# A GEGLU layer in seven block products: thirteen column pairs in place of twelve, four pairs' first products made ahead, some weight sums on GpSimd

## The chip, the cores and the metric

The kernel runs on one core of one Trainium2 chip. The metric is the time of one execution in microseconds (us); lower is better. Beside it stands the *span* of the profile, from the first to the last instruction that the trace shows. Three engines matter: TensorE (PE; its weight loads are PEld), VectorE (DVE) and ScalarE (ACT). GpSimd (POOL) is idle in the kernel before, but for 0.7 us at the start.

## The reference, cut to what matters

```python
B, S, D, F = 32, 32, 1024, 3584          # 1024 tokens in all, bf16
def reference(x, w_gate, w_up, w_down):
    return (gelu_tanh(x @ w_gate) * (x @ w_up)) @ w_down
```

## The kernel before

A product of 2 x 2 blocks is usually eight block products. The Winograd form needs seven, and some sums of blocks. The kernel uses it in the first layer (tokens in two halves of 512, D in two halves, two column tiles of 128 as a *pair*) and in the second.

- Products 1 and 2 use unsummed blocks in bf16. Products 3 to 7 use sums, kept as fp32r, a four-byte float type. Every matmul is 128x128 by 512 columns. A *slot* is one product, four matmuls. Matmuls write to PSUM, a memory of eight *banks*, of 512 columns each here; the other tiles lie in SBUF.
- A pair (gate and up) takes 14 products, 56 matmuls: 16 in bf16, 40 in fp32r. Without sums it would take 64.
- Four of 28 column tiles are computed directly, in two passes of 64 matmuls, one per half of the tokens. The second pass is *cover*: VectorE makes the sums of x meanwhile.
- `at=` is no time on the chip. It only sorts each engine's queue. TensorE's queue stands in program order. Waits on semaphores follow from reads and writes of the tiles.

```python
        KO = 2
        for h in range(2):                       # the direct tiles: one pass per half
            ...                                  # 64 matmuls each, then GELU and product
        # sums of x: DVE; the unsummed block S4 is converted by ACT
        sums_x(0, 21)
        sums_x(1, 23.5)
        sums_x(2, 26)
        sums_x(3, 28)
        sums_x(4, 32)
        ...                                      # the five weight blocks of pair 0
        for p in range(NP):                      # NP = 12
            ...
            product(1, 0, A[0], True)            # product n, gate (0) or up (1), PSUM bank
            act(bank(B[0]), bank(A[0]), COPY, at(1))
            product(1, 1, A[1], True)
            act(bank(B[1]), bank(A[1]), COPY, at(2))
            product(5, 0, E[0], True)
            act(p5[0], bank(E[0]), COPY, at(3))
            product(2, 0, A[0], False)
            act(g11, bank(A[0]), GELU, at(4))
            product(2, 1, A[1], False)
            glu(ml, 0, g11, bank(A[1]), at(5.2))
            product(6, 0, B[0], False)
            act(bank(C[0]), bank(B[0]), COPY, at(6))
            product(6, 1, B[1], False)
            act(bank(C[1]), bank(B[1]), COPY, at(7))
            product(5, 1, E[1], True)
            ...                                  # products 7, 3, 7, 3, 4, 4; adds, GELUs, products
            if p + 1 < NP:                       # weight sums of the next pair, all but one on DVE
                for u in range(3):
                    sums_w(p + 1, u, at(0.5 + 1.5 * u + (5.5 if p == 0 else 0)))
                sums_w(p + 1, 3, at(8.5))
                sums_w(p + 1, 4, at(7 if p else 9.05))
        ...                                      # second layer: seven sweeps of 56 matmuls
```

## Time and profile before

| | before |
|---|---|
| time, median (range of 4 runs) | 277.11 us (276.85 to 277.46) |
| span of the profiled run | 275.9 us |
| matmuls with the weights (bf16 + fp32r) | 432 + 760 |

First, the page's busy table (share of the span, number of instructions) and its chain of work that ended last.

```profile
## 1 busy us (share of the span) xinstructions
PE 270.6 (98%) x1191; PEld 184.4 (67%) x1208; DVE 208.2 (75%) x234; ACT 118.1 (43%) x180; POOL 0.7 (0%) x6
...
## 4 chain that ended last, share of the span: by engine, by line
PE 95%; DMA 2%; issue 1%; SPq 0%; DVE 0%
```

TensorE binds. The matmul records are long (0.38 to 0.40 us) and overlap, so their sum is no cost. Weight loads are the better ruler. There is one for each matmul, none is missing (1208), and the order of the program says which one belongs to which product. Counted so, an undisturbed bf16 matmul takes 0.2158 us (the second pass: 64 in 13.81 us), and an fp32r one 0.2267 us (a sweep of the second layer: 56 in 12.69 us). This is the ruler for all stage times. After a wait the first loads run a little ahead of their matmuls, so a stage border is good to about 0.2 us. Where fp32r products give way to bf16 ones the shift is regular: in a later pair the loads of the first product take 0.66 us, not 0.86, and those of the last product of the pair in front 1.13, not 0.91.

Next, the weight loads in order of time: start, length, and in brackets the idle time before with what ended it. Of the tiles, `arena` holds x and unsummed weights, `S` the sums of x, `T` those of the weights, `tmp` intermediates, `hT` the hidden layer; `ps` is PSUM. The four lines at the top are the first pass (the fourth runs on into what follows), the next four the first pair, the last is product 5 of the second pair.

```profile
4.58 1.44 PEld L117 LDWEIGHTS ps<-arena 128*128 128x128 bf16 x8 [0.28 <-issue]
6.69 1.41 PEld L117 LDWEIGHTS ps<-arena 128*128 128x128 bf16 x8 [0.67 <-DMA arena<-in_w_gate_dram]
8.75 1.42 PEld L117 LDWEIGHTS ps<-arena 128*128 128x128 bf16 x8 [0.64 <-issue]
10.75 23.87 PEld L117 LDWEIGHTS ps<-arena 128*128 128x128 bf16 x112 [0.58 <-issue]
...
34.73 0.86 PEld L117 LDWEIGHTS ps<-S,T 128*128 128x128 f32 x4
36.02 1.41 PEld L117 LDWEIGHTS ps<-arena 128*128 128x128 bf16 x8 [0.42 <-ACT ps L117]
...
44.23 0.76 PEld L117 LDWEIGHTS ps<-S,T 128*128 128x128 f32 x4 [0.35 <-DVE tmp L117]
45.43 0.77 PEld L117 LDWEIGHTS ps<-S,T 128*128 128x128 f32 x4 [0.44 <-DVE tmp L117]
...
47.99 0.87 PEld L117 LDWEIGHTS ps<-S,T 128*128 128x128 f32 x4
```

The groups of eight in the first pass start 2.0 to 2.1 us apart where eight matmuls need 1.73: TensorE waits for first data. In pair 0 it waits once for a ScalarE copy and twice for VectorE. At the start VectorE has the sums of two pairs to make. Product 5 of pair 0 starts at 34.73 us and that of pair 1 at 47.99: 13.26 us, where later pairs repeat every 12.61. So the first pair loses 0.65 us. Its 13.46 us in the ledger below hold 0.2 more, because it follows bf16 matmuls and lacks the head start of a later pair.

Then the busy time by window: length, then busy us of each engine with its instructions, clock, DMA share and GB/s. The windows are pair 0, pair 1 and pair 2.

```profile
core 0: us, PE busy (x) PEld busy (x) DVE busy (x) ACT busy (x) POOL busy (x), PEclk, DMA share, GB/s
...
33.00:46.46 13.46, 13.40 (x57) 8.85 (x56) 13.32 (x16) 10.05 (x15) 0.00 (x0) 1.00 0.29 78
46.46:59.08 12.62, 12.55 (x56) 8.92 (x57) 10.61 (x14) 6.93 (x11) 0.00 (x0) 1.00 0.67 177
59.08:71.68 12.60, 12.53 (x56) 8.92 (x56) 10.06 (x13) 6.93 (x11) 0.00 (x0) 1.00 0.43 137
```

In pair 0 VectorE is busy 13.32 of 13.46 us. In a later pair TensorE has the time to itself: 12.61 us, where 56 matmuls at cadence are 12.52.

Last, two groups of instructions: out<-in, shapes, count, busy us, mean ns.

```profile
L117 PE MATMUL ps<-S,T 128*128 128x512 f32 x480 | 118.4, 400 | 0.0
...
L117 DVE TENSOR_TENSOR T<-arena,T 128x1024 fp32r<-128x1024 bf16 x38 | 46.2, 1222 | 11.5 <-PE ps L117 11.1
```

One weight sum on VectorE is 1.22 us. The Trainium skill (VectorE: DVE Perf Modes, "The TRN2 errata") gives (N+151)/0.96 ns for an fp32 add of two tensors, checked there at N = 512 and 2048. My estimate from it for N = 1024 is 1224 ns. The trace agrees (1222), for a difference of bf16 blocks written as fp32r.

### The profile page before, as it was taken

What the parts mean: (1) busy time and instruction counts of PE and PEld (TensorE: products, weight loads), DVE (VectorE), ACT (ScalarE), POOL (GpSimd) and SP (SyncE); (2) the same over time, 40 slices, a digit from 0 to 9 for tenths busy, and PEclk for the clock granted to TensorE, in tenths of its full rate; (3) what the DMA queues carried; (4) which work ended last, traced back from release to release, by engine and by line L of the source; (5) the groups of instructions that cost most, each with busy time, mean ns of one, the idle gap of its engine ahead of it and who ended that gap; (6) DMA issues with size and microseconds to landing.
All of it is one profiled execution on the core that took longest, in us unless ns stands there. A gap on an engine that the chain in (4) does not pass through costs nothing.

```text
span 275.9 us, 3173 instructions
## 1 busy us (share of the span) xinstructions
PE 270.6 (98%) x1191; PEld 184.4 (67%) x1208; DVE 208.2 (75%) x234; ACT 118.1 (43%) x180; POOL 0.7 (0%) x6
## 2 busy tenths in 40 slices
PE   8999999999999999999999999999999999999995
PEld 3344466767686867677676868674447888888884
DVE  1049799896969678887969696269971999999942
ACT  2030484646454645556464546431121122245551
POOL 1000000000000000000000000000000000000000
PEclk9999999999999999999999999999999999999999
DMA  7999550593082029006700700194011000001112
GB/s 160 253 222 295 147 142 2 155 318 99 0 238 69 0 58 249 0 0 163 183 0 0 229 2 0 50 333 151 0 38 38 0 2 0 1 0 61 38 57 76
DMA packets 44815, 26.42 MB, mean 96 GB/s; under 512 B 8448, under 2 KB 44800, under 8 KB 44800
## 3 DMA queue, kind: packets, MB, share of 16 engines
q1 hardware_dynamic: 42576, 24.25, 32.2%
q10 hardware_dynamic: 2224, 1.97, 2.9%
q8 instruction: 9, 0.15, 0.2%
q14 instruction: 6, 0.05, 0.1%
HBM read 22.28 MB, written 2.10 MB: 88 GB/s over the span
## 4 chain that ended last, share of the span: by engine, by line
PE 95%; DMA 2%; issue 1%; SPq 0%; DVE 0%
PE ps L117 95%; DMA arena<-in_x_dram 2%; SPq L117 0%; DVE arena L117 0%
## 5 line engine op out<-in xcount | busy, mean ns | idle before, releaser
L117 PE MATMUL ps<-S,T 128*128 128x512 f32 x480 | 118.4, 400 | 0.0
L117 PEld LDWEIGHTS ps<-S,T 128*128 128x128 f32 x480 | 90.0, 188 | 21.5 <-DVE tmp L117 0.8
L117 PE MATMUL ps<-arena 128*128 128x512 bf16 x306 | 71.1, 379 | 1.4 <-DMA arena<-in_w_gate_dram 0.2
L117 ACT ACTIVATE tmp<-ps 128x512 f32<-128x512 f32 x64 | 38.3, 598 | 69.7 <-PE ps L117 69.5
L117 PEld LDWEIGHTS ps<-arena 128*128 128x128 bf16 x320 | 29.2, 98 | 39.9 <-issue 4.4
L117 ACT ACTIVATE ps<-ps 128x512 f32<-128x512 f32 x56 | 32.4, 581 | 52.6 <-PE ps L117 50.2
L117 DVE TENSOR_TENSOR T<-arena,T 128x1024 fp32r<-128x1024 bf16 x38 | 46.2, 1222 | 11.5 <-PE ps L117 11.1
L117 DVE TENSOR_TENSOR T<-arena 128x1024 fp32r<-128x1024 bf16 x38 | 45.8, 1217 | 7.4 <-PE ps L117 7.4
L117 PE MATMUL ps<-T,S 128*128 128x512 f32 x224 | 51.3, 390 | 0.0
L117 PEld LDWEIGHTS ps<-T,S 128*128 128x128 f32 x224 | 42.0, 188 | 8.8
L117 DVE TENSOR_TENSOR tmp<-ps,tmp 128x512 f32<-128x512 f32 x48 | 32.9, 689 | 12.9 <-PE ps L117 12.9
L117 DVE TENSOR_TENSOR hT<-tmp,ps 128x512 bf16<-128x512 f32 x32 | 21.8, 684 | 19.8 <-PE ps L117 19.8
L117 PE MATMUL ps<-arena,hT 128*128 128x512 bf16 x109 | 24.0, 379 | 0.2
L117 PEld LDWEIGHTS ps<-arena,hT 128*128 128x128 bf16 x112 | 10.9, 98 | 13.2 <-issue 0.3
L117 DVE TENSOR_TENSOR hT<-tmp 128x512 bf16<-128x512 f32 x24 | 16.6, 692 | 2.5
L117 ACT ACTIVATE tmp<-tmp 128x512 f32<-128x512 f32 x24 | 15.1, 632 | 6.9 <-DVE tmp L117 6.0
L117 DVE TENSOR_TENSOR S<-hT 128x1024 fp32r<-128x1024 bf16 x14 | 16.5, 1217 | 0.0
L117 PE MATMUL ps<-S 128*128 128x512 f32 x56 | 12.9, 389 | 0.0
L117 ACT ACTIVATE T<-arena 128x1024 fp32r<-128x1024 bf16 x12 | 12.6, 1053 | 0.0
L117 PEld LDWEIGHTS ps<-S 128*128 128x128 f32 x56 | 10.5, 188 | 2.2
L117 ACT ACTIVATE S<-arena 128x1024 fp32r<-128x1024 bf16 x9 | 9.3, 1055 | 3.2 <-PE ps L117 3.0
L117 ACT ACTIVATE S<-hT 128x1024 fp32r<-128x1024 bf16 x7 | 7.2, 1056 | 5.5 <-PE ps L117 5.5
(23 smaller groups left out, 48.3 us busy)
## 6 DMA issues: line engine op xcount, KB each, us to landing
arena<-in_w_gate_dram SPq DMA_DIRECT2D x12, 512.0 KB, 5.3
arena<-in_w_up_dram SPq DMA_DIRECT2D x12, 512.0 KB, 7.1
arena<-in_w_down_dram SPq DMA_DIRECT2D x4, 1536.0 KB, 8.3
out_dram<-arena SPq DMA_DIRECT2D x12, 128.0 KB, 1.7
arena<-in_w_down_dram SPq DMA_DIRECT2D x4, 256.0 KB, 6.6
arena<-in_w_up_dram ACTq DMA_DIRECT2D x4, 128.0 KB, 5.4
arena<-in_w_gate_dram ACTq DMA_DIRECT2D x2, 256.0 KB, 5.7
arena<-in_w_up_dram ACTq DMA_DIRECT2D x2, 256.0 KB, 6.2
```

Source lines behind the costliest of these rows:

```text
L117: ins = name(eng, *args, **kw) if callable(name) else getattr(eng, name)(*args, **kw)
```

## The change

Two direct tiles become a thirteenth pair. That would leave half the cover for the sums of x, so products 1 and 2 of four pairs run ahead of the pairs: those of pairs 0 and 1 inside the first pass, those of pairs 2 and 3 as 32 matmuls after a shorter second pass. Product 1 alone is needed later, so ScalarE saves its PSUM bank to SBUF (`kept`, in tiles of the hidden layer not written yet) before product 2 is added, and restores it when the pair comes. These four *early* pairs then have 10 slots, the nine *late* ones 14. GpSimd makes the first weight sum of each next pair, and in late pairs the third too. Two intermediates move from SBUF to PSUM. The matmuls with the weights go from 1192 to 1184.

```diff
-        BASE, PAIR = 32.0, 12.6
-        NP = 12
+        LEFT = [11, 12] + list(range(11))
+        NP, EARLY = len(LEFT), 4
+        kept = [hT[:, m:m + 2, :].rearrange("p t n -> p (t n)").bitcast(FP32).rearrange("p (j n) -> p j n", j=2)
+                for m in (7, 9, 22, 24)]
...
+            if k == 3 and m < 2:
+                act(kept[m][:, j, :], bank(2 * m + j), COPY, 10.5)
...
+        for p in (2, 3):
+            at = 25.8 + (p - 2) * 3.46
+            g, u = 2 * p, 2 * p + 1
+            for b, j, k0 in ((g, 0, 0), (u, 1, 0), (g, 0, 4), (u, 1, 4)):
+                for k in range(k0, k0 + 4):
+                    mm(b, stat(p, j, k), x0[:, k, :], k == 0, k in (3, 7), add=k > 3)
+                if k0 == 0:
+                    act(kept[p][:, j, :], bank(b), COPY, at + 0.9 * (j + 1))
+            act(tmp[:, p, :], bank(g), GELU, at + 2.7)
+            tt(hT[:, left(p), 0:512], tmp[:, p, :], bank(u), MUL, at + 3.6)
...
-        sums_x(4, 32)
+        sums_x(4, 22)
...
+            if p < EARLY:
+                o = -4
+                for j in range(2):
+                    act(bank(B[j]), kept[p][:, j, :], COPY, at(0.1 + j * 0.1))
+                product(5, 0, E[0], True)
+                act(p5[0], bank(E[0]), COPY, at(1))
+                product(5, 1, E[1], True)
+                product(6, 0, B[0], False)
+                act(bank(C[0]), bank(B[0]), COPY, at(3))
+                act(p5[1], bank(E[1]), COPY, at(3.1))
+                product(6, 1, B[1], False)
+                act(bank(C[1]), bank(B[1]), COPY, at(4))
...
+            u22 = bank(A[1] if p < EARLY - 1 else E[1])
...
-                for u in range(3):
-                    sums_w(p + 1, u, at(0.5 + 1.5 * u + (5.5 if p == 0 else 0)))
-                sums_w(p + 1, 3, at(8.5))
-                sums_w(p + 1, 4, at(7 if p else 9.05))
+                sums_w(p + 1, 0, at(o + 9), "pool", [t4])
+                if p + 1 < EARLY:
+                    sums_w(p + 1, 1, at(o + 11.5))
+                    sums_w(p + 1, 2, at(o + 14.3))
+                    sums_w(p + 1, 3, at(o + 9.5))
+                    t4 = sums_w(p + 1, 4, at(o + 14.4))
+                else:
+                    sums_w(p + 1, 1, at(o + 14.3))
+                    sums_w(p + 1, 2, at(o + 12), "pool")
+                    sums_w(p + 1, 3, at(o + 9.5))
+                    t4 = sums_w(p + 1, 4, at(o + 20.5))
```

The cuts hold the loading order (right-hand weights of pairs 0 and 1, then weights of pairs 2 and 3, then the rest), the first-pass columns (1408 to 1919 in place of 0 to 511) and the renumbering of tiles.

## The prediction

> **What bounds the kernel now.** TensorE. The busy table gives it 98% of 275.9 us at a granted clock of 1.00; the chain that ended last is 95% TensorE. Windows of the pair stage show it busy 12.53 of each 12.6 us, VectorE 10.06, ScalarE 6.9. From starts in the timeline I read a cadence of 0.228 us per fp32r matmul (sweep stage: 280 between 209.15 and 272.98 us) and about 0.216 per bf16 one. At these, 760 fp32r and 432 bf16 matmuls are 266.4 of the 268.4 us from the first weight matmul (4.61) to the last. Of the other 2 us, about 1.0 is waiting for the first DMAs (starts at 4.61, 6.70, 8.78, not 1.73 apart) and 0.65 lies in the first pair (product 5 at 34.76, the next pair's at 48.02: 13.26 us; later pairs repeat every 12.61), behind late ScalarE copies and VectorE sums. Only matmul count and these 2 us can be won.
>
> **What the change does.**
> - Two direct column tiles become a thirteenth pair: 64 bf16 matmuls before, 16 bf16 and 40 fp32r after. That is 48 bf16 fewer, 40 fp32r more: -10.36 + 9.12 = **-1.24 us**, all on the critical path.
> - Half the cover for the x sums (32 matmuls of the second half) goes; 32 matmuls (products 1 and 2 of pairs 2, 3) replace it; those of pairs 0 and 1 fall out of the first pass. The pairs should start near 33.0 us as before, with sums ready: **-0.3 to -0.6 us** of the first pair's stall.
> - ScalarE gains 8 saves and 8 restores of 0.58 us: 9.3 us on an engine 43% busy. Each save must end before its accumulation goes on; for pairs 2 and 3 the slack is about 0.1 us.
> - VectorE hands 21 weight sums to GpSimd but gets a pair. An early pair lasts 10 slots, 9.05 us, with 3 sums of 1.22 and 7 passes of 0.69: 8.5 us, 94%, the tight place. A late pair needs 8.0 of 12.6.
> - GpSimd: the trace has no such operation. The Trainium skill (GPSIMD Engine Reference, section 3.1) gives 4497 ns for 2048 fp32 elements with two inputs; my estimate for 1024 is 2.3 us. SBUF — State Buffer, "Who interferes with whom", says that a VectorE operation with two SBUF inputs and a GpSimd operation that reads SBUF exclude each other. The diff answers it: GpSimd sums follow the last VectorE sum, beside passes with a PSUM operand. This trace shows neither. I expect little blocking and **+0 to +1 us** of stalls, in the early pairs.
> - DMA: about the same bytes. First weights of pairs 2 and 3 must land by 26 us; at that stretch's 290 GB/s I estimate 25.
>
> The down stage is unchanged.
>
> **Prediction: 275.7 us**, 8 in 10 between 274.7 and 277.5. Faster by over 2%: 0.01; within 2%: 0.96; slower by over 2%: 0.03.
>
> **What would show it.** Right: late pairs repeat every 12.6 us, early ones every 9.1 to 9.3; sweeps start about 1.5 us earlier; VectorE busy near 190 us, GpSimd near 50 in operations of 2.3. Wrong: early pairs over 9.4 us, TensorE waiting for the VectorE sum behind a GpSimd one; VectorE sums stretched well beyond 1.22 us (blocking); TensorE idle near 26 us (DMA) or between 10 and 14 (saves).
>
> **What would make it wrong.** GpSimd at 4 us or more for an operation: each early pair would lose up to 1 us behind the sum that needs its result, and the time would be 277 to 279. Or early-pair orders on VectorE so tight that banks come free late. A gain over 2 us has no source in this profile.

## The result, and the profile after

| | before | after |
|---|---|---|
| time, median (range of 4 runs) | 277.11 us (276.85 to 277.46) | 276.09 us (275.81 to 276.64) |
| ratio, 95% interval | | 0.9965 (0.9944 to 0.9985) |
| span of the profiled run | 275.9 us | 274.7 us |

A ratio is the mean time of one kernel's fast runs over that of the other's in the same rounds, so it is not quite the ratio of the medians.

The busy table and the chain of the kernel after:

```profile
## 1 busy us (share of the span) xinstructions
PE 269.5 (98%) x1186; PEld 187.4 (68%) x1200; DVE 189.8 (69%) x221; ACT 126.1 (46%) x195; POOL 45.5 (17%) x27
...
## 4 chain that ended last, share of the span: by engine, by line
PE 96%; DMA 2%; issue 0%; DVE 0%; ACTq 0%
```

The chain is TensorE as before. Its weight loads in order of time: first pass, matmuls ahead, two early pairs.

```profile
8.76 1.42 PEld L117 LDWEIGHTS ps<-arena 128*128 128x128 bf16 x8 [0.59 <-issue]
10.50 2.29 PEld L117 LDWEIGHTS ps<-arena 128*128 128x128 bf16 x12 [0.32 <-issue]
13.84 14.36 PEld L117 LDWEIGHTS ps<-arena 128*128 128x128 bf16 x68 [1.05 <-DMA arena<-in_w_up_dram]
...
32.04 0.55 PEld L117 LDWEIGHTS ps<-arena 128*128 128x128 bf16 x4 [0.32 <-ACT hT L117]
32.90 0.55 PEld L117 LDWEIGHTS ps<-arena 128*128 128x128 bf16 x4 [0.32 <-ACT hT L117]
...
46.62 8.96 PEld L117 LDWEIGHTS ps<-S,T 128*128 128x128 f32 x40 [0.25 <-issue]
55.82 8.93 PEld L117 LDWEIGHTS ps<-S,T 128*128 128x128 f32 x40 [0.25 <-issue]
```

The wait at 13.84 is new and is for weights of the first pass. The saves (`ACT hT`) show idle PEld of 0.32 us, but matmuls queue behind each other: the 32 ahead took 6.98 us in all, 0.07 over cadence. Busy time by window, columns as before, of two early pairs (1 and 2) and two late ones (4 and 5):

```profile
42.78:51.98 9.20, 9.20 (x41) 7.43 (x40) 7.97 (x11) 6.01 (x11) 2.16 (x1) 1.00 0.43 116
51.98:61.16 9.18, 9.18 (x41) 7.43 (x40) 7.97 (x11) 6.02 (x11) 2.15 (x1) 1.00 0.87 261
...
70.56:83.17 12.61, 12.54 (x56) 8.93 (x56) 7.63 (x11) 6.93 (x11) 4.25 (x2) 1.00 0.33 82
83.17:95.78 12.61, 12.54 (x56) 8.92 (x56) 7.63 (x11) 6.93 (x11) 4.25 (x2) 1.00 0.42 110
```

The groups that answer to those shown of before:

```profile
L117 PE MATMUL ps<-S,T 128*128 128x512 f32 x520 | 125.5, 398 | 0.0
...
L117 POOL TENSOR_TENSOR T<-arena 128x1024 fp32r<-128x1024 bf16 x21 | 44.8, 2151 | 123.4 <-DVE T L117 114.7
...
L117 DVE TENSOR_TENSOR T<-arena,T 128x1024 fp32r<-128x1024 bf16 x40 | 48.5, 1219 | 0.0
```

A GpSimd sum is 2.15 us, and VectorE sums keep their 1.22: the two were kept apart in time. The ledger from the weight loads:

| stage of TensorE | before, us | after, us | at cadence, before / after |
|---|---|---|---|
| first pass, 64 matmuls | 14.61 | 15.10 | 13.81 / 13.81 |
| second pass; or second pass and ahead, 64 | 13.81 | 13.89 | 13.81 / 13.81 |
| all pairs | 152.14 | 150.46 | 150.25 / 148.96 |
| of these pair 0 | 13.46 | 9.21 | 12.52 / 9.07 |
| second layer, 392 matmuls | 87.5 | 87.5 | 87.6 / 87.6 |

The pairs gained 1.68 us: 1.29 by the matmul count and 0.38 by all else, chiefly shorter waits. The first pass lost 0.49. That loss was the first thing to settle: an accident, or the change?

### The profile page after: what moved, and what is told of

Read it like the earlier page. It is cut to its first block, busy times and chain, and to the rows that moved or that the text cites. A ratio compares the mean times of both kernels' runs of the same rounds, so it can differ in the third digit from the quotient of the medians.

```text
span 274.7 us, 3245 instructions
## 1 busy us (share of the span) xinstructions
PE 269.5 (98%) x1186; PEld 187.4 (68%) x1200; DVE 189.8 (69%) x221; ACT 126.1 (46%) x195; POOL 45.5 (17%) x27
## 4 chain that ended last, share of the span: by engine, by line
PE 96%; DMA 2%; issue 0%; DVE 0%; ACTq 0%
PE ps L117 96%; DMA arena<-in_w_up_dram 2%; DVE arena L117 0%; ACTq L117 0%
## 5 line engine op out<-in xcount | busy, mean ns | idle before, releaser
L117 PE MATMUL ps<-S,T 128*128 128x512 f32 x520 | 125.5, 398 | 0.0
L117 PEld LDWEIGHTS ps<-S,T 128*128 128x128 f32 x520 | 97.4, 188 | 22.7 <-issue 0.8
L117 POOL TENSOR_TENSOR T<-arena 128x1024 fp32r<-128x1024 bf16 x21 | 44.8, 2151 | 123.4 <-DVE T L117 114.7
L117 DVE TENSOR_TENSOR hT<-tmp,ps 128x512 bf16<-128x512 f32 x56 | 37.2, 686 | 39.2 <-PE ps L117 36.8
L117 PE MATMUL ps<-arena 128*128 128x512 bf16 x261 | 60.7, 381 | 1.5 <-DMA arena<-in_w_up_dram 0.6
L117 DVE TENSOR_TENSOR T<-arena,T 128x1024 fp32r<-128x1024 bf16 x40 | 48.5, 1219 | 0.0
L117 PEld LDWEIGHTS ps<-arena 128*128 128x128 bf16 x272 | 24.7, 98 | 34.7 <-issue 4.5
L117 DVE TENSOR_TENSOR tmp<-ps,tmp 128x512 f32<-128x512 f32 x26 | 18.0, 692 | 21.9 <-PE ps L117 21.9
L117 DVE TENSOR_TENSOR T<-arena 128x1024 fp32r<-128x1024 bf16 x19 | 22.7, 1222 | 7.5 <-PE ps L117 7.4
L117 DVE TENSOR_TENSOR ps<-ps,tmp 128x512 f32<-128x512 f32 x30 | 20.9, 696 | 2.8 <-PE ps L117 2.8
```

The lines of the kernel that those rows point to most:

```text
L117: ins = name(eng, *args, **kw) if callable(name) else getattr(eng, name)(*args, **kw)
```

## The experiments

**Theory A**: the gain is the count plus shorter waits, and the first pass's 0.49 us is an accident of when data landed. **Theory B**: the change slows the first pass. **Rivals on the waits**: GpSimd's relief of VectorE is what made them shorter, against order alone.

### e0_after_again: the changed kernel as it is

> The changed kernel itself, unaltered, as control. Theory A (the first pass lost 0.49 us in the profiled run by an accident of when weights landed): over more rounds the mean gain against before is about 1.5 us, and this profile's first pass (64 matmuls, 14.61 us before, 15.10 us in the first profile after) varies by some tenths of a us between profiles, in either direction. Theory B (the change itself slows the first pass): gain about 1.0 us again and a first pass near 15.1 us again. Both: the pair stage is again 150.5 us (before 152.1).

Measured: 276.17 us, ratio 0.9953 (0.9936 to 0.9971), a gain of 1.3 us on the means. The first pass took 13.66 us this time, 1.4 less than in the first profile after. All pairs took 150.44. But the fast first pass was not all kept:

```profile
25.53 0.55 PEld L117 LDWEIGHTS ps<-arena 128*128 128x128 bf16 x4 [0.51 <-DMA arena<-in_w_gate_dram]
26.43 0.55 PEld L117 LDWEIGHTS ps<-arena 128*128 128x128 bf16 x4 [0.36 <-DMA arena<-in_w_up_dram]
```

At 25.5 us TensorE was ready for the matmuls ahead and their weights were not there; second pass and ahead took 14.14 us instead of 13.81. So the first pass is an accident, in both directions (theory A), and the change has one new meeting point with the DMA that the kernel before, whose second pass uses weights long landed, has not.

### e8_first_columns_0: the old columns in the first pass (wrong result)

```diff
-            dma(eng, first[:, j, k0:k1, :], w_r[j][:, k0:k1, F0 * P:(F0 + 4) * P], ...)
+            dma(eng, first[:, j, k0:k1, :], w_r[j][:, k0:k1, 0:512], ...)
```

> The changed kernel, but the first weight loads read columns 0 to 511 as before instead of 1408 to 1919 (a wrong result, on purpose; same sizes and order). Theory A: first pass and time as in the control, within 0.3 us. Theory B in the form 'other columns land later': first pass back to about 14.6 us, 0.4 to 0.5 us faster than the control.

Measured: 276.08 us, ratio 0.9955 (0.9938 to 0.9972), as the control. First pass 14.56 us; second pass and ahead 14.31. The time does not follow the columns, so theory B in this form falls. Over all fourteen traces the first pass took 13.63 to 15.10 us: 14.2 to 14.6 in the three with the old tiling, and on both sides of that with the new one. Pair 0 started at 32.8 to 33.0 us in the three with the old tiling, and at 32.2 to 33.6 in the ten with four pairs ahead.

### e10_before_gpsimd: the GpSimd part alone, on the kernel before

```diff
-                for u in range(3):
-                    sums_w(p + 1, u, at(0.5 + 1.5 * u + (5.5 if p == 0 else 0)))
-                sums_w(p + 1, 4, at(7 if p else 9.05))
+                sums_w(p + 1, 0, at(9), "pool", [t4])
+                sums_w(p + 1, 1, at(14.3))
+                sums_w(p + 1, 2, at(12), "pool")
+                t4 = sums_w(p + 1, 4, at(20.5))
# and u22, u12 in PSUM banks
```

> The kernel before with the GpSimd part alone: two of the four weight sums of pairs 1 to 11 on GpSimd, the last sum late in the next pair, two intermediates in PSUM; four direct tiles and twelve pairs as before. If the first pair's loss (13.46 us, later pairs 12.61) comes from VectorE having the sums of two pairs to make in it, this wins 0.6 to 0.8 us of it and the later pairs stay at 12.61. The rival, that this loss comes from ScalarE (its copies wait behind the conversion of x), leaves 13.2 us or more. GpSimd busy about 47 us, which by itself buys nothing in the steady pairs.

The edit also moves the sums to a later place in the order; e12 below separates the two. Measured: pair 0 fell from 13.46 to 12.94 us, a little less than expected, and later pairs stayed at 12.61. So the rival, ScalarE, has at most the rest. But the time did not fall: 277.45 us, ratio 1.0007 (0.9992 to 1.0023). The mean span was 274.92 us against 275.45 of before in the same rounds, 0.53 less, as the trace says. The measured time less the span was 2.54 us in every run (2.51 to 2.57) against 1.78. The gain inside was eaten by 0.76 us outside the span.

### e7_both_orders: two orders altered in the changed kernel

```diff
-        for p in (2, 3):                 # a save has 4 matmuls to end
-            for b, j, k0 in ((g, 0, 0), (u, 1, 0), (g, 0, 4), (u, 1, 4)):
+        for k0 in (0, 4):                # a save has 16 matmuls to end
+            for p in (2, 3):
+                for b, j in ((g, 0), (u, 1)):
...
-                product(5, 1, E[1], True)
                 product(6, 0, B[0], False)
-                act(bank(C[0]), bank(B[0]), COPY, at(3))
-                act(p5[1], bank(E[1]), COPY, at(3.1))
+                act(bank(C[0]), bank(B[0]), COPY, at(2))
+                product(5, 1, E[1], True)
+                act(p5[1], bank(E[1]), COPY, at(3))
```

> The changed kernel with two orders altered: the 32 matmuls of pairs 2 and 3 that run ahead alternate between the two pairs, so a save has 16 matmuls to end instead of 4; in early pairs product 6 of gate comes before product 5 of up, so its PSUM copy has 8 matmuls instead of 4. I expect 0.07 us from the first (6.98 us for the 32, 6.91 at cadence) and 0.1 us in each of four early pairs from the second (9.20 us, 9.07 at cadence): together 0.3 to 0.5 us faster than the control. Rival: the 0.14 us in an early pair is VectorE or GpSimd being late, and then the order changes nothing or makes it worse.

Measured: 275.92 us, ratio 0.9945 (0.9927 to 0.9963), not separable from the control. The trace does separate them: pairs 1 and 2 took 9.067 us each, the cadence to the last digit, where the control had 9.18. Its loads run through these pairs without a gap that the view would split; the control has one of 0.25 us in each:

```profile
37.91 24.21 PEld L117 LDWEIGHTS ps<-S,T 128*128 128x128 f32 x107
```

So the rest of an early pair was the copy from bank B to bank C, with only one product to hide behind. Pair 0 lost 0.16 us (9.38, where the control had 9.22). In its trace the second restore starts at 34.70 us, after ScalarE has waited 1.67 us for VectorE's products of the matmuls ahead, and TensorE waits 0.25 us for ScalarE and then 0.31 for a VectorE sum. Both of these VectorE products now start at 33.98 us or later; in the control the first was done at 32.22. The altered order of the matmuls ahead makes the first one later. Net gain of the early pairs 0.18 us: less than expected, for that reason.

### e2_early_sums_on_dve and e3_late_sums_on_dve: GpSimd's sums back on VectorE, one half each

```diff
# e2
-                sums_w(p + 1, 0, at(o + 9), "pool", [t4])
+                sums_w(p + 1, 0, at(o + 9), "dve" if p + 1 < EARLY else "pool", [t4])
# e3
-                sums_w(p + 1, 0, at(o + 9), "pool", [t4])
+                sums_w(p + 1, 0, at(o + 9), "pool" if p + 1 < EARLY else "dve", [t4])
-                    sums_w(p + 1, 2, at(o + 12), "pool")
+                    sums_w(p + 1, 2, at(o + 14.4))
```

> The changed kernel with the first weight sum of pairs 1 to 3 back on VectorE (pairs 4 to 12 keep GpSimd). VectorE then needs 9.7 us in an early pair that TensorE does in 9.07. If GpSimd is what lets the early pairs run at TensorE's pace, pairs 0 to 2 together take 1 to 2 us more than the control's 27.6 us. Rival: VectorE can spread the load, because three early pairs are few and it starts ahead; then under 0.3 us more.

> The changed kernel with both GpSimd sums of pairs 4 to 12 back on VectorE (18 operations; pairs 1 to 3 keep GpSimd). VectorE then needs 10.4 of 12.6 us in a late pair, as in the kernel before (12.61 us per pair). I expect the late pairs to stay at 12.61 us and the time as in the control: there GpSimd moves work off an engine that does not bind. Rival: VectorE becomes late in the order it has now, and late pairs lengthen by 0.1 us or more. The part of the measured time outside the span (1.78 us before, 2.00 in the control, 2.54 with GpSimd sums in the kernel before) should fall towards 1.8 if each GpSimd operation adds to it; if it stays, its number is not what counts.

Measured: 275.72 us, ratio 0.9947 (0.9923 to 0.9971), and 275.79 us, ratio 0.9944 (0.9916 to 0.9972). Neither lost anything. In e2 pairs 0 to 2 took 27.65 us, against 27.58 in the control: my expectation of 1 to 2 us more failed. Its error was the sum. I had added up record lengths, but VectorE records overlap: two sums of 1.22 us start 1.13 apart, passes of 0.69 about 0.60. The windows view counts overlap once. For early pair 1 of e2 (the window's columns as above) it says:

```profile
42.19:51.40 9.21, 9.21 (x42) 7.43 (x40) 9.01 (x12) 5.98 (x11) 0.00 (x0) 1.00 0.36 100
```

VectorE is busy 9.01 of 9.21 us and still in time. In e3 late pairs stayed at 12.61 us, as expected. The part outside the span was 1.82 and 1.78 us in these two (means), with 18 and 3 GpSimd sums; the control, with 21, had 2.00.

### e4_pool_any_time: GpSimd's sums not kept apart from VectorE's

```diff
-                sums_w(p + 1, 0, at(o + 9), "pool", [t4])
+                sums_w(p + 1, 0, at(o + 9), "pool")
```

> The changed kernel without the order that makes GpSimd's first sum of a pair wait for VectorE's last sum of the pair before: GpSimd runs it as soon as its buffer is free, beside VectorE sums with two SBUF inputs. If the two exclude each other as the skill's page says, VectorE sums or GpSimd sums stretch (a VectorE sum of 1.22 us to as much as 3.4, or a GpSimd one from 2.15 upwards), and early pairs, where VectorE has 0.5 us to spare, lengthen by 0.5 us or more each; late pairs stay at 12.61. Rival: no exclusion for these operations; all durations stay and so does the time.

Measured: 278.7 us, ratio 1.0055 (1.0029 to 1.0081): slower than before, by 1.4 us on the means. Pairs 1 to 3 took 10.21, 10.16 and 10.44 us, a full us more each; late pairs 12.61. In the timeline, from pair 0 into pair 1:

```profile
40.22 0.70 DVE L117 TENSOR_TENSOR ps<-ps,tmp 128x512 f32<-128x512 f32 x1 [0.21 <-PE ps L117]
40.35 2.14 POOL L117 TENSOR_TENSOR T<-arena 128x1024 fp32r<-128x1024 bf16 x1 [11.47 <-PE ps L117]
40.82 2.75 DVE L117 TENSOR_TENSOR T<-arena,T 128x1024 fp32r<-128x1024 bf16 x1
...
43.50 0.68 DVE L117 TENSOR_TENSOR hT<-tmp,ps 128x512 bf16<-128x512 f32 x1
...
45.60 0.60 ACT L117 ACTIVATE ps<-hT 128x512 f32<-128x512 f32 x1 [2.49 <-DVE hT L117]
...
46.26 0.76 PEld L117 LDWEIGHTS ps<-S,T 128*128 128x128 f32 x4 [1.06 <-ACT ps L117]
```

The VectorE sum starts 0.47 us after GpSimd's and ends at 43.57, 1.08 us after GpSimd's end at 42.49. It ran when GpSimd was done. So did all twelve VectorE sums that began during a GpSimd sum: each ended 1.08 or 1.09 us after it. Of the GpSimd sums, two began during a VectorE sum and grew from 2.15 to 3.16 and 2.54 us. The VectorE sum at 40.82 does not wait for GpSimd's result: the sum that it reads was begun at 25.7 us and done at 28.9, and the wait is inside the instruction, not in front of it. This agrees with the Trainium skill, SBUF — State Buffer, "Who interferes with whom": a VectorE instruction with two SBUF inputs and a GpSimd one that reads SBUF exclude each other. The sum's delay of 1.5 us passes to the VectorE products behind it, these free their PSUM banks late, ScalarE makes the second restore late (it waited 2.49 us), and TensorE waits 1.06 us for ScalarE. In the table of waits (total us, times, longest us) this is the first line for PEld:

```profile
PEld ps L117 <- ACT ps L117: 5.6, 12, 1.1
```

In the control the same line has 2.5 us in 9 waits (both from 24 to 190 us). So the order in the change, GpSimd after VectorE's last sum, is worth about 2.8 us to a kernel that uses GpSimd (the two ratios differ by 0.0102).

### e11_sbuf_operands: the two intermediates back in SBUF

```diff
-            u22 = bank(A[1] if p < EARLY - 1 else E[1])
+            u22, u12 = tmp[:, 6, :], tmp[:, 7, :]
-            tt(bank(B[1]), bank(B[1]), p5[1], ADD, at(o + 12.1))
-            glu(mr, 0, g12, bank(B[1]), at(o + 13))
+            tt(u12, bank(B[1]), p5[1], ADD, at(o + 12.1))
+            glu(mr, 0, g12, u12, at(o + 13))
```

> The changed kernel with two intermediates back in SBUF, so that in each pair two VectorE products have two SBUF inputs again, and in late pairs they fall beside GpSimd sums. If they exclude each other, these products wait up to 1.5 us more in a late pair or GpSimd's sums grow beyond 2.15 us; late pairs have slack for that, so the time changes by under 0.5 us. Rival: no exclusion, products stay at 0.69 us and GpSimd sums at 2.15.

Measured: 276.14 us, ratio 0.9961 (0.9939 to 0.9983), pairs as in the control. All instances of the product with two SBUF inputs (min, median, max in ns):

```profile
L117 DVE TENSOR_TENSOR hT<-tmp x26: 683/693/1612, 41.1 to 182.6; 128x512 bf16<-128x512 f32 x26
...
67.70 1.61 DVE L117 TENSOR_TENSOR hT<-tmp 128x512 bf16<-128x512 f32 x1
```

The median is unchanged. In most pairs the two hardly met: in late pair 4, GpSimd's second sum ended at 80.26 us and the product started at 80.31. Only two of the 26 products began during a GpSimd sum, and just these were stretched: the one at 67.70, to 1.61 us, beside a GpSimd sum that ended at 68.76, and one at 143.34, to 0.88, beside one that ended at 143.67. Each ended about 0.55 us after GpSimd's sum. So exclusion shows here too, where the two meet. The time shows that the move to PSUM bought nothing at this order.

### e5_two_ahead: only two pairs ahead

```diff
-        NP, EARLY = len(LEFT), 4
+        NP, EARLY = len(LEFT), 2
-        for p in (2, 3):                 # and the 32 matmuls ahead are gone from here
```

What depends on `EARLY` changes with it: pairs 2 and 3 get their sums in the order of late pairs, with two on GpSimd.

> The changed kernel with only two pairs running ahead (those in the first pass); pairs 2 and 3 make products 1 and 2 in their turn, so 32 matmuls move from before pair 0 to after it. The matmul count is the same. If running ahead is cover for VectorE's sums of x and of the first weights and saves nothing by itself, pair 0 starts about 6.9 us earlier and then TensorE waits for the fourth x sum, which ended near 35 us: I estimate 3.5 to 6 us more than the control in all. Rival: running ahead matters little, since pairs need their sums one after the other; then within 1 us of the control.

Measured: 279.8 us, ratio 1.0086 (1.0053 to 1.0118), so about 3.7 us more than the control by the two ratios (0.0133 of 277.4). Pair 0 started at 26.59 us and took 11.62 us, pair 1 took 9.96; cadence is 9.07. TensorE waited for sums:

```profile
31.95 0.76 PEld L117 LDWEIGHTS ps<-S,T 128*128 128x128 f32 x4 [1.74 <-DVE T L117]
33.08 0.30 PEld L117 LDWEIGHTS ps<-S,T 128*128 128x128 f32 x2 [0.38 <-DVE S L117]
34.22 6.67 PEld L117 LDWEIGHTS ps<-S,T 128*128 128x128 f32 x30 [0.84 <-DVE S L117]
```

The estimate of 3.5 to 6 us held. So running ahead saves no work. It is the cover that the two given-up direct tiles used to be, and without it the thirteenth pair costs more than it wins.

### e12_before_sum_order: order alone, on the kernel before

```diff
-        sums_x(4, 32)
+        sums_x(4, 22)
-                for u in range(3):
-                    sums_w(p + 1, u, at(0.5 + 1.5 * u + (5.5 if p == 0 else 0)))
-                sums_w(p + 1, 4, at(7 if p else 9.05))
+                sums_w(p + 1, 0, at(9))
+                sums_w(p + 1, 1, at(14.3))
+                sums_w(p + 1, 2, at(14.4))
+                sums_w(p + 1, 4, at(20.5))
```

> The kernel before with order changes alone, no GpSimd: sums of the next pair after the products of this one (the last of them in the next pair), and ScalarE's x conversion 10 us earlier in its order. Four direct tiles, twelve pairs. If the first pair's 0.85 us over the 12.61 of later pairs was only order, pair 0 falls from 13.46 to 12.6-12.7 us, the later pairs stay at 12.61, and the time falls by 0.5 to 0.9 us against before. Rival: VectorE needs GpSimd's help there (which gave 12.94), and pair 0 stays above 13.2.

Measured: 276.74 us, ratio 0.9967 (0.9948 to 0.9986). Pair 0 fell to 12.82 us, later pairs stayed at 12.61. The waits of PEld from 32 us to 47.5 (before) and to 47 (this kernel):

```profile
PEld ps L117 <- DVE tmp L117: 0.8, 2, 0.4
PEld ps L117 <- ACT ps L117: 0.4, 1, 0.4
...
```

```profile
PEld ps L117 <- ACT ps L117: 0.3, 1, 0.3
PEld ps L117 <- issue: 0.3, 1, 0.3
```

The waits for VectorE are gone without GpSimd and without a thirteenth pair. What is left stands in every later pair too. From product 5 of pair 0 (34.53 us) to that of pair 1 (47.14) it is 12.61 us, so order alone took away the whole 0.65; the 0.2 by which pair 0 still seems longer is the border. With GpSimd (e10) the same distance was 12.74. e10 had not the earlier conversion of x, so the two parts of this edit are not separated.

### e13_orders_no_gpsimd: both orders of e7, no GpSimd sum at all

```diff
-                sums_w(p + 1, 0, at(o + 9), "pool", [t4])
+                sums_w(p + 1, 0, at(o + 9))
-                    sums_w(p + 1, 2, at(o + 12), "pool")
+                    sums_w(p + 1, 2, at(o + 14.4))
```

> The kernel with both altered orders, and all weight sums on VectorE: no GpSimd sum at all. From the two runs that put half of them back without loss I expect early pairs at 9.07 to 9.2 us and late ones at 12.61, and the time at or 0.2 us below that of the two orders with GpSimd (275.9 us), as the part outside the span was 1.8 instead of 2.0 us in some kernels. Rival: with both halves back VectorE is late somewhere and pairs 3 to 5 lengthen by 0.2 us or more.

Measured: 275.05 us, ratio 0.9914 (0.9893 to 0.9935), below the interval of the change in e0_after_again (0.9936 to 0.9971) by a hair. Pairs 1 and 2 took 9.067 us, late pairs 12.61, and the part outside the span was 1.78 us. So GpSimd's sums are not needed. That the time falls by leaving them out is not shown: the fair comparison is e7, with the same two orders, and its interval (0.9927 to 0.9963) overlaps that of e13. The parts that were measured are small: all pairs 150.09 us against 150.26, and outside the span 1.78 against 2.07.

### e14_weights_first: and the weights for the matmuls ahead first

```diff
-        load_near(10)
-        load_pairs(1, 0, 11, slice(0, 4))
+        load_pairs(1, 0, 10, slice(0, 4))
+        load_near(10.5)
...
+        sums_x(2, 24.5)
-        sums_w(0, 0, 24.5)
-        sums_w(0, 1, 27)
-        sums_x(2, 28)
+        sums_w(0, 0, 27)
+        sums_w(0, 1, 28)
```

> As the kernel without GpSimd, and the first half of the weights for the 32 matmuls that run ahead is loaded before the right-hand weights of pairs 0 and 1 instead of after them, with the third x sum before the first weight sum on VectorE. In four of six profiles TensorE waited 0.2 to 0.6 us for those weights near 26 us. I expect that wait gone: second pass plus ahead 13.82 us in every profile (14.1 to 14.3 where it waited), pair 0 not later than 32.3 us plus the first pass's own delay, and 0.2 to 0.4 us less than the kernel without GpSimd on average. Rival: bytes decide, not their order, and another wait takes its place in pair 0.

Measured: 275.27 us, ratio 0.9921 (0.9901 to 0.9941). In the trace the waits near 26 us are gone: from 9.97 us to pair 0 the weight loads run without a gap that the view would split.

```profile
9.97 22.14 PEld L117 LDWEIGHTS ps<-arena 128*128 128x128 bf16 x104 [0.46 <-issue]
32.23 1.78 PEld L117 LDWEIGHTS ps<-S,T 128*128 128x128 f32 x8
```

Second pass and ahead took 13.81 us, and pair 0 started at 32.23, the earliest of all traces. The time is not below that of e13: a difference of 0.2 us between six runs each cannot be told from the first pass's own spread of over 1 us. That this order wins time is not shown; that it removes the wait is, in one trace.

## Why the prediction was right, and where it was off

The predicted time was 275.7 us; 276.09 was measured, and 276.17 in the control. The predicted gain was about 1.4 us, the measured one 1.0 and 1.3 (means of the two sets of rounds).

- **Count**: -1.24 predicted, -1.29 in the ledger (40 x 0.2267 - 48 x 0.2158). Right. A pair that replaces 64 direct matmuls wins only 1.2 us, since 40 of its 56 matmuls run at the slower fp32r cadence and each late pair is 0.09 us over its cadence.
- **First pair's stall**: sized as 0.65 us, and the trace has 0.65. The prediction had -0.3 to -0.6 of it; all of it went. Its reason, late ScalarE copies and VectorE sums, is what order alone removed in the old kernel (e12).
- **Early pairs**: "+0 to +1 us of stalls" was predicted, and about 0.5 came (0.11 to 0.14 in each early pair). That was the right place and size with the wrong reason, so luck. I put it to GpSimd and to VectorE at 94%. The experiments show the copy between PSUM banks (e7), and VectorE able to take one more sum per pair (e2).
- **The sum of the two**: pair 0 of before was 0.85 over a later pair (0.65 and 0.2 of border). The early pairs are 0.73 over their cadence (0.5 and 0.2 of border), and three late pairs fewer save 0.26, which I had not counted. Net -0.38.
- **GpSimd**: 2.3 us per sum estimated from the skill's 4497 ns for 2048 elements, 2.15 measured; no blocking in the change, as predicted (VectorE sums 1.22 us, as before). That GpSimd is off the critical path was right. That it was not needed at all (e2, e3, e13) I had not seen.
- **Saves**: slack of 0.1 us predicted for pairs 2 and 3. The 32 matmuls took 0.07 us more than cadence: nearly right.
- **DMA**: weights of pairs 2 and 3 "must land by 26 us; I estimate 25". This step failed in part. In five of the nine traces with the change's loading order TensorE waited for them, and second pass and matmuls ahead took 0.2 to 0.5 us over cadence (e0, e4, e7, e8, e11); the waits in e3 and e13 cost 0.1 or less. The first profile, with a first pass of 15.10 us, shows no such wait. But e8 waited after one of 14.56, and e2 did not after one of 14.42, so the speed of the first pass alone does not decide it.
- **Not in the prediction**: time outside the span. It grew from 1.78 us to 2.00. That is 0.2 us of loss, where the gain fell short by 0.1 to 0.5. What sets it stays open: kernels without GpSimd sums had 1.8 us every time, those with them 1.8 (e2, e3, e4), 2.0 to 2.1 (the change, e5, e7, e8, e11) or 2.5 (e10), and the number of GpSimd sums does not order them.
- **Second layer**: unchanged, as predicted; 87.5 us both times.

## What to carry to other kernels

When TensorE is at 98%, price a change in matmuls times their own cadence, read from starts, and look for the few waits at stage boundaries: here order alone won as much in the old kernel as the whole change did at first (ratios 0.9967 and 0.9965). Work moved to an idle engine bought nothing here, since with the sums in another order the engine that it left was not late. Test that by putting it back, and count an engine's load by windows, not by adding up records that overlap.

## What the Trainium skill lacked or had wrong

- TensorE: Matmul & The Clock Gate has no cadence for fp32r matmuls. Here: 0.2267 us for 512 columns against 0.2158 in bf16, 5% more.
- GPSIMD Engine Reference, section 3.1, has its two-input time for fp32 alone. Here: 2.15 us for 1024 elements, bf16 in and fp32r out, a little less than half of its 4497 ns for 2048.
- SBUF — State Buffer, "Who interferes with whom", agrees with e4 (a sum of 1.22 us became 2.75) and e11 (a product of 0.69 became 1.61). It does not say where a profile shows the wait: here inside the blocked instruction's record, with no idle time in front of it.
- No page has that the measured time outside the profile's span depends on the program: 1.78 to 1.80 us without GpSimd sums, 1.78 to 2.54 with them.
